# One written table for the order, the PSUM banks and the SBUF cells of an attention-and-MLP kernel

## The chip, the cores and the metric

The kernel runs on one core of one Trainium2 chip. The metric is the device time of one execution in microseconds (us). Three executions of the kernel before the change gave 410.02, 409.84 and 410.39 us; their median, 410.02 us, is the time before. The core has five instruction streams that run beside each other and meet only at semaphores: PE (TensorE, matrix products), ACT (ScalarE), DVE (VectorE), POOL (GpSimd) and SP (SyncE, which only issues DMAs here).

## The reference

A layer norm feeds a 16-head self-attention and a GELU MLP; the MLP, through SiLU, gates the attention's output, and the input is added. There are 2048 tokens of 448 numbers, heads of 28, and 1792 hidden columns. All inputs are bf16.

```python
xn = (x - mean(x)) / sqrt(var(x) + 1e-5)
qkv = (xn @ wqkv).reshape(B, S, 3, 16, 28)            # -> q, k, v by head
p = softmax(einsum("bhqd,bhkd->bhqk", q, k) * 28 ** -0.5)
s = einsum("bhqk,bhkd->bhqd", p, v) @ wo              # heads put side by side first
g = silu(gelu(xn @ w1 + b1, approximate=True) @ w2 + b2)
return x + s * g
```

## The kernel before, in words

**Scores.** The scores are cut into 1024 tiles of 128 keys by 512 queries, numbered m = 0 to 1023. A block is 64 tiles: one of four groups of four heads and one of four chunks of 512 queries; block b = m // 64, and m % 4 is the head in its group. PE makes a tile with a 32-row product, and four of these, one for each head, can stand side by side in PE's rows: this is a *row phase*. All other products of the main part use PE's columns: four products of 32 columns each side by side, a *slot*. A padded score tile (`p_alone`) is made in column mode, with a query operand that is zero for the other heads, and needs no change of mode. Changing between rows and columns costs PE time.

**Banks.** A product lands in PSUM, in one of eight banks that the program calls `ring`. Score tiles, projections, transposes and the accumulators of P·V all share these eight. A bank is free when what it holds has been read.

**Exponentials.** They are made on two engines.
- ScalarE reads two or three banks in one ACTIVATE (a *pair* or a *triple*) and writes bf16 to *cells* of P. Cells lie in several tensors whose first contents are dead by then, so in the profile they carry the names P, h, xnT and others.
- VectorE takes *groups* of four tiles with the same keys. A first pass (one `tensor_scalar` for each tile, multiply and add, written as uint16) makes bit patterns that are approximately the exponential. Two shifted copies of the whole group (128x2048, an integer added) follow, and P·V uses all three with weights of their own (`vs` holds the weighted V). A shifted copy is one DVE instruction (`tensor_scalar` on 128x2048 uint16) or two halves on POOL (`tensor_tensor` on 128x512 int32 with `shc`). The two copies can be *added* into one, which saves P·V a use: as one DVE instruction, or as accumulating DMAs that POOL issues (`p_expq`).

**P·V and the rest.** `t_pv` multiplies P with V, four heads a slot, and accumulates a block in one bank. When the bank is wanted elsewhere, or at the block's end, DVE moves the accumulator out (*evacuation*, `p_pv`, `p_epi`). Through the kernel's length the other work is spread between these: projections to q, k, v and to the MLP's hidden columns, whose last 64 rows are done either as full products or as two 32-row products that join a row phase ("joined"), GELU and tanh on ACT, SiLU by DVE and POOL (`p_silu`), the output projection and the output DMAs.

**The order.** `run` is a greedy scheduler with a cost model; it makes one list of operations (some 3,100 of them, numbered in order), each with its engine, the function that issues it, and `need`, the operations it must follow: R (reads what they wrote), W and A (overwrites what they wrote or read), X, and P and Q for the port. [...] `arrange` then permutes each engine's list by `ORD`: each number says how many of the remaining operations to step over. `place` sets the bank of some uses of banks by `BANKS` and works out the waits on banks anew, and `emit_all` writes each engine's program, with a semaphore wait ahead of an operation where its engine has not already waited for as much. `filler` puts products of `ident` and `zero` on PE where the scheduler sees nothing to do. A helper (line 258, in `_Eng`) issues every instruction, so nearly all profile lines have L258, and one goes by the names of tiles and by shapes.

**Beginning and end.** In the head, x and the weights come by DMA, and the statistics of the first four x tiles are made on DVE (`p_ln`) and, for tile 3, on ACT (`p_sums`: a copy that sums, operation 43, and a square that sums, 56). `p_ln2` makes the logarithm and the root for tiles 0 and 1 (half 0: operations 50, 53) and for 2 and 3 (half 1: 65, 69) on ACT, and the normalised tiles on DVE (58, 60 and 75, 72). PE transposes these; the transposed halves are copied out on ACT and DVE, `p_q0` makes the first q, and then the first scores can start. In the tail, `t_ones` and a reciprocal finish the softmax's sums of the last block, and the last outputs are multiplied, added and sent by SP, POOL and ACT.

Of the kernel before, what the change touches and what calls it, by code (L numbers as in the profile page):

```python
# [14 lines left out]
ORD = {  # L15
# [70 lines left out]
    ),  # L86
}
TO = ()
BANKS = {
# [9 lines left out]
H = 16  # L99
# [2933 lines left out]
```

## Time and profile before

| | |
|---|---|
| time of three runs | 410.02, 409.84, 410.39 us (median 410.02) |
| span of the profiled execution | 408.0 us, so 2.0 us of the median lie outside it |
| busy: PE, ACT, DVE, POOL | 395.1, 398.1, 343.5, 194.8 us |
| granted PE clock | 9 (tenths, 90% or more) in all 40 slices of the span |
| first exponential starts | 12.58 us |
| last exponential ends | 401.90 us |
| last DMA issued | 405.52 us |

The span is cut by these rows into a head of 12.6 us, a middle of 389.3 us in which ScalarE and VectorE make the exponentials, and a tail of 6.1 us. Busy time is the sum of the instructions' own durations with overlaps counted once; on PE and ACT an instruction starts before the one ahead of it has left the pipeline, so being busy isn't the same as having no time to spare, and the distance from one start to the next says more.

### The profile page before, as it was taken

The numbers are of one execution on the slowest core, as the hardware profiler recorded it, in microseconds if no ns is written. First come the engines' busy times: TensorE is split into PE (matmuls) and PEld (weight loads), VectorE is DVE, ScalarE is ACT, GpSimd is POOL, SyncE is SP. The second block draws the span as 40 slices with busy tenths as digits, with TensorE's granted clock in tenths as the row PEclk, the third lists the DMA queues.
The fourth block names the chain that finished last, engine by engine and source line by source line (L and its number), as shares of the span: only waits on it lengthen the run. The fifth ranks groups of instructions, "written<-read, shape, count | busy, mean of one in ns | idle before, by whom it ended". The sixth has DMA issues, their size and how long they took to land.

```text
span 408.0 us, 14601 instructions
## 1 busy us (share of the span) xinstructions
PE 395.1 (97%) x6157; PEld 144.6 (35%) x6157; DVE 343.5 (84%) x596; ACT 398.1 (98%) x409; POOL 194.8 (48%) x221
## 2 busy tenths in 40 slices
PE   6899999999999999999999999999999999999996
PEld 5443233333332333332223444332333323333363
DVE  8967688896679889989898127999998999798976
ACT  5999999999999999999999999999999999999995
POOL 7595457649982563254652231156156013555041
PEclk9999999999999999999999999999999999999999
DMA  8902110000101010100331100220010003200065
GB/s 244 305 2 42 4 31 2 16 20 19 29 3 31 2 25 11 34 2 2 77 116 30 30 3 6 55 53 15 18 34 2 4 31 57 64 20 21 14 114 134
DMA packets 18783, 17.54 MB, mean 43 GB/s; under 512 B 8941, under 2 KB 15421, under 8 KB 18686
## 3 DMA queue, kind: packets, MB, share of 16 engines
q1 hardware_dynamic: 16734, 13.55, 12.0%
q0 software_dynamic: 1008, 2.49, 3.8%
q8 instruction: 48, 0.79, 0.9%
q10 hardware_dynamic: 976, 0.57, 0.5%
q14 instruction: 17, 0.14, 0.1%
HBM read 12.54 MB, written 2.88 MB: 38 GB/s over the span
## 4 chain that ended last, share of the span: by engine, by line
PE 59%; ACT 28%; issue 7%; DVE 4%; DMA 1%; POOL 0%; ACTq 0%; DVEq 0%; POOLq 0%
PE ring L258 59%; ACT P L258 16%; ACT h L258 8%; ACT xnT L258 3%; DVE st L258 1%; DVE h L258 1%; DVE xnT L258 1%; DMA x_sb<-in_A_x_dram 1%; DVE vaug L258 0%; DVE x_sb L258 0%; ACT w L258 0%; DVE qT L258 0%; POOL h L258 0%; DVE mv L258 0%; DVE w L258 0%
## 5 line engine op out<-in xcount | busy, mean ns | idle before, releaser
L258 ACT ACTIVATE P<-ring 128x1024 bf16<-128x1024 f32 (+1 forms) x236 | 253.8, 1246 | 1.0 <-PE ring L258 1.0
L258 PE MATMUL ring<-qT,kT 32*128 32x512 bf16 (+2 forms) x1131 | 131.7, 359 | 4.2 <-ACT P L258 1.0
L258 ACT ACTIVATE h<-ring 128x1024 bf16<-128x1024 f32 (+2 forms) x93 | 101.3, 1204 | 2.0 <-PE ring L258 2.0
L258 PEld LDWEIGHTS ring<-qT,kT 32*128 32x128 bf16 x1131 | 36.3, 91 | 121.8 <-ACT P L258 48.1
L258 DVE TENSOR_SCALAR vaug<-ring 128x512 uint16<-128x512 f32 x92 | 60.8, 683 | 5.5 <-PE ring L258 4.8
L258 PE MATMUL ring<-xnT,w 128*32 128x512 bf16 (+1 forms) x880 | 65.3, 381 | 0.0
L258 PE MATMUL ring<-w,h 128*32 128x448 bf16 x896 | 58.5, 356 | 0.0
L258 PE MATMUL ring<-P,vaug 128*32 128x512 bf16 (+2 forms) x606 | 57.9, 351 | 0.2
L258 POOL TENSOR_TENSOR qT<-x_sb,E_sb 128x512 bf16<-128x512 f32 x15 | 17.4, 1162 | 64.6 <-DMA x_sb<-recs 38.0
L258 ACT ACTIVATE xnT<-ring 128x1024 bf16<-128x1024 f32 (+2 forms) x41 | 47.6, 1199 | 0.5 <-PE ring L258 0.5
L258 POOL TENSOR_TENSOR rc<-rs,mone 128x16 f32<-128x16 bf16 x11 | 33.3, 3023 | 28.7 <-DMA rs<-E_sb 14.6
L258 DVE TENSOR_SCALAR w<-ring 128x512 uint16<-128x512 f32 x52 | 34.5, 683 | 2.0 <-PE ring L258 1.7
L258 PEld LDWEIGHTS ring<-xnT,w 128*32 128x32 bf16 (+1 forms) x880 | 21.7, 96 | 28.0 <-issue 6.6
L258 PEld LDWEIGHTS ring<-w,h 128*32 128x32 bf16 x896 | 19.3, 95 | 24.4 <-issue 14.8
L258 PE MATMUL ring<-h,vaug 128*32 128x512 bf16 x201 | 25.1, 383 | 0.0
L258 PE MATMUL ring<-xnT,wq 128*32 128x512 bf16 (+2 forms) x240 | 22.6, 379 | 0.2 <-DVE w L258 0.2
L258 PEld LDWEIGHTS ring<-P,vaug 128*32 128x32 bf16 x606 | 17.3, 95 | 13.6 <-issue 7.4
L258 PE MATMUL ring<-xnT,wk 128*32 128x512 bf16 (+2 forms) x244 | 21.8, 379 | 0.3 <-DVE xnT L258 0.2
L258 DVE TENSOR_SCALAR h<-ring 128x512 uint16<-128x512 f32 x28 | 18.9, 685 | 3.3 <-PE ring L258 3.0
L258 POOL TENSOR_TENSOR qsq<-qT 128x512 bf16<-128x512 bf16 x12 | 13.0, 1079 | 17.0 <-DVE x_sb L258 13.9
L258 DVE CAST qT<-ring 128x512 bf16<-128x512 f32 x15 | 10.3, 688 | 12.7 <-PE ring L258 12.7
L258 DVE CAST h<-ring 128x512 bf16<-128x512 f32 x24 | 16.5, 688 | 4.8 <-PE ring L258 4.8
(207 smaller groups left out, 616.8 us busy)
## 6 DMA issues: line engine op xcount, KB each, us to landing
x_sb<-recs SPq DMA_DIRECT2D x60, 64.0 KB, 2.1
w<-in_B_w_dram SPq DMA_DIRECT2D x1, 1568.0 KB, 7.3
w<-in_B_w_dram SPq DMA_DIRECT2D x1, 1344.0 KB, 8.7
x_sb<-in_A_x_dram SPq DMA_DIRECT2D x2, 448.0 KB, 6.6
out_dram<-in_A_x_dram SPq DMA_DIRECT2D x2, 448.0 KB, 10.6
out_dram<-h POOLq DMA_DIRECT2D x4, 224.0 KB, 4.6
out_dram<-h SPq DMA_DIRECT2D x7, 112.0 KB, 4.4
xnT<-wq POOLq DMA_DIRECT2D x1, 512.0 KB, 6.6
```

What stands on the lines that cost most here:

```text
L258: return lambda *a, **k: f(*[real(x) for x in a], **{n: real(x) for n, x in k.items()})
```

## The change

One string, `PLAN`, with 3,586 entries, replaces `ORD`, `TO` and `BANKS`. It gives the order on all engines at once, the banks, and the cells that the exponentials go to. `run` still makes its list; operations that the plan names by number (`R`) are kept, with the bank that the plan gives. For the core of the work `arrange` makes the operations anew from the entries:

| entry | makes | before | after |
|---|---|---|---|
| X m,m(,m)/cells | exponential on ACT of one, two or three banks, of any equal spacing | 354 (286 pairs, 68 triples), 776 tiles | 358 (280 pairs, 67 triples, 11 singles), 772 tiles |
| S, C | score tile, padded score tile | 21 padded | 11 padded |
| A | first pass of a group's tile on DVE | 248 (62 groups) | 252 tiles (63 groups), 4 pairs of banks taken in one instruction |
| H, G | shifted copy on DVE, half of one on POOL | 92 and 64 | 54 and 144 |
| M | addition of two copies on DVE | 2, and 3 by DMA | 13 |
| V | product with V | 375 slots | 369 slots |
| E | evacuation of a P·V accumulator on DVE | 34 | 29 |
| P, J, Q | a projection's full products, its joined rests, its evacuation | 14 joined | 16 joined |

The waits come from a record of who last used each bank, cell and group place in the order of the plan (`take`, `room`, `begin`, `touch`). The fillers and the additions by DMA are dropped. DMA loads on SP and ACT keep their order. A POOL operation that wants the port waits for the last DVE operation in the plan's order that wants it. `emit_all` keeps for each operation only the largest wait of each semaphore. On ACT and DVE the first operations stand in another order (before: 43, 50, 53, 56, 65, 69, ...; after: 50, 53, 43, 56, 71, 65, 69, ...; on DVE before: 38, 42, 46, 52, 48, 58, ..., after: 38, 42, 46, 58, 60, 48, 52, ...), and at the end the last tanh (operation 3071) stands ahead of the last eight exponentials, and the output DMA 3075 ahead of 3062.

```diff
-ORD = {
-    'PE': (
-        0, 0, 0, 0, 0, 0, 0, 0, 0, 0, 0, 0, 0, 0, 0, 2, 2, 2, 0, 1, 1, 0, 19, 19, 1, 18, 2, 0, 0, 1, 3, 4, 0, 0, 0, 1, 0, 1, 0, 0, 0, 0, 0, 0, 3, 1,
...
-TO = ()
-BANKS = {
...
+PLAN = """
+    R2 R15 R16 R0 R4 R5 R6 R7 R3 R1 R35/7 R17 R38 R8 R21 R22 R264 R9 R24 R25 R26 R294 R18 R36/7 R19 R37/7 R42 R20 R39/7 R46 R40/7 R41/7 R44/7 R23
...
+    X803,804/0,16 V780,0/5 S895/3 S806/2 S805/1 S888/4 X805,806/1,4 A895/21 V816,0/5 V820,1/5 R2473 S890/0 S808/6 S807/7 R2544/3 R2545/3 X808,807/2,6
...
+    R3058/0 R3068/5 X1022,1023/10,13 R3059/0 R3064/0 R3070/4 R3081/1 R3072/4 R3073/4 R3065/2 R3082/1 R3066/2 R3076/5 R3085/1 R3086 R3037 R3069/0
+    R3079/4 R3084/5 R3088 R3074 R3067/2 R3087/2 R3083/0 R3089/2 R3090/0 R3093 R3091/0 R3031 R3054 R3025 R3075 R3062 R3094 R3092
+"""
...
+            elif t == "X":
+                bs = [sc[m][1] for m in a]
+                st = bs[1] - bs[0] if len(bs) > 1 else 1
+                src, dst = K.ring[:, bs[0]:bs[-1] + 1:st, :], cells(at)
+                need = [("R", H(sc[m][0])) for m in a]
+                for c in at:
+                    need += room([K.b_P[c]], cell, c)
+                o = new(ACT, lambda eng, src=src, dst=dst: eng.activation(dst, src, ACTF.Exp, scale=SM_SCALE), need, ("exp", a))
...
+            if o.port and o.E == POOL and port is not None:
+                o.need.append(("P", H(port)))
+            if o.port and o.E == DVE:
+                port = o
...
+                most = {}
                 for kind, (s, c) in o.need:
                     p = find[(id(s), c)]
-                    if kind == "Q" or kind == "P" and E == DVE or kind != "X" and E == PE and p.sem is self.evsem[PE]:
+                    if kind == "P" and E == DVE or kind != "X" and E == PE and p.sem is self.evsem[PE]:
                         continue
                     if done.get(id(p.sem), 0) < p.cnt:
                         done[id(p.sem)] = p.cnt
-                        self.prog[E].append(lambda eng, s=p.sem, c=p.cnt: eng.wait_ge(s, c))
+                        most[id(p.sem)] = p
+                for p in most.values():
+                    self.prog[E].append(lambda eng, s=p.sem, c=p.cnt: eng.wait_ge(s, c))
```

More of the change, by code (lines that the diff above doesn't have):

```diff
@@ L441, in arrange @@
-    def arrange(self):
-        seq = {}
-        for x in TO:
-            (self.to if len(x) > 2 else self.join)(*x)
-        self.chain_up()
-        for E, name in ((PE, "PE"), (ACT, "ACT"), (DVE, "DVE"), (POOL, "POOL"), (SP, "SP")):
-            lst = [o for o in self.ops if o.E == E]
-            at, left = [], list(range(len(lst)))
-            for d in ORD.get(name, ()):
-                at.append(left.pop(d))
-            seq[E] = [lst[i] for i in at + left]
-        self.place(seq)
-        self.emit_all(seq)
@@ L542, in chain_up @@
-    def chain_up(self):
-        chain = [o for o in self.ops if o.port and o.start is not None]
-        for at, o in sorted(self.put_port[::-1], key=lambda x: -x[0]):
-            chain.insert(at, o)
-        last = {}
-        for o in chain:
-            for E, kind in ((POOL if o.E == DVE else DVE, "P"), (o.E, "Q")):
-                if E in last:
-                    o.need.append((kind, (last[E].sem, last[E].cnt)))
-            last[o.E] = o
+        of = lambda h: K.by_h[(id(h[0]), h[1])]
@@ new lines, in arrange, with kind @@
+        K.number()
+        name = lambda o: o.fn.__qualname__.split(".<locals>.")[0].split(".")[-1] + ("" if o.fn.__qualname__.endswith("<lambda>") else "." + o.fn.__qualname__.split(".")[-1])
+        evac = {o.spec[1]: o for o in K.ops if o.spec and o.spec[0] == "ev" and not (o.spec[1][0] == "qk" and o.spec[1][2] == 0)}
+        keys = sorted(evac, key=str)
+        core = ("s", "sc", "exp", "a", "h", "evac", "last")
+        def kind(o):
+            s = o.spec
+            if name(o) == "filler.f" or o.kind == "x" or name(o) == "p_expq" and s is None:
+                return "gone"
+            if not s:
+                return "rest"
+            if s[0] == "pv":
+                return "rest" if s[2][0][0] // 64 == NBLK - 1 else "core"
+            if s[0] in core:
+                return "core"
+            if s[0] in ("pr", "ev") and s[1] in evac:
+                return s[0]
+            return "rest"
@@ new lines, in arrange @@
+        final = {o.spec[1]: o for o in K.ops if o.spec and o.spec[0] == "last"}
+        plan = [(x[0], *([int(z) for z in y.split(",") if z] for y in x[1:].split("/"))) for x in PLAN.split()]
+        ops, seq = {o.no: o for o in K.ops}, {E: [] for E in (PE, ACT, DVE, POOL, SP)}
+        full = {x[1][0] for x in plan if x[0] == "P" and x[1][1] == KT - 1}
+        merged = {x[1][0] for x in plan if x[0] == "M"}
+        grouped = {x[1][0] // 4 * 4 for x in plan if x[0] == "A"}
+        left = [sum(1 for x in plan if x[0] == "V" and x[1][0] // 64 == b) for b in range(NBLK)]
@@ new lines, in through @@
+        def through(p):
+            c, s = kd[id(p)], p.spec
+            if c == "rest" or c == "ev":
+                return [p]
+            if c == "pr":
+                return [evac[s[1]]]
+            if c == "core" and s[0] == "last":
+                return [p]
+            if c == "core" and s[0] in ("s", "sc", "pv"):
+                b = (s[1] if s[0] != "pv" else s[2][0])[0] // 64
+                return [final[b]] if b in final else []
+            return []
+        was = {id(o): list(o.need) for o in K.ops}
@@ new lines, in arrange @@
+        K.ops = [o for o in K.ops if kd[id(o)] == "rest" or o in list(evac.values()) or o in list(final.values())]
+        bank = {i: [] for i in range(NRING)}
+        cell, lane = {}, {}
+        sc, ex, ap, sh, pads, acc, burst, begun, part = {}, {}, {}, {}, {}, {}, {}, {}, set()
+        pr, done, last_pad, port, e1 = {}, set(), [], None, None
+        pad_of = [o for o in K.ops if name(o) == "p_pad" and o.E == SP]
+        shc = [o for o in K.ops if name(o) == "p_pad.f"][0]
+        vs = {o.spec[1:]: o for o in K.ops if o.spec and o.spec[0] == "vs"}
@@ new lines, in new, with take, cells @@
+        def new(E, fn, need, spec, port=False):
+            K.n_new += 1
+            o = K.op(E, fn, (K.evsem[E], 10 ** 6 + K.n_new), 1, (), (), "t", 0.1, 0.05, "", (), port, spec=spec)
+            o.need += need
+            return o
+        def take(i):
+            need = [("A" if p.E != PE else "W", H(p)) for p in bank[i]]
+            bank[i] = []
+            return need
+        def cells(cs):
+            reg, k = K.pslots[cs[0]]
+            n = len(cs)
+            st = cs[1] - cs[0] if n > 1 else 1
+            return reg[:, k:k + st * (n - 1) + 1:st, :]
@@ new lines, in used, with room @@
+        def used(x):
+            return [("A", H(p)) for p in [p for p in x if not p.spec or p.spec[0] not in ("exp", "a")] or x]
+        def room(toks, at, key):
+            if key in at:
+                return used(at[key])
+            need, seen = [], set()
+            for b in toks:
+                for h in first.get(id(b), ()):
+                    for p in through(of(h)):
+                        if id(p) not in seen:
+                            seen.add(id(p))
+                            need.append(("A", H(p)))
+            return need
@@ new lines, in touch, with score @@
+        def touch(u, o):
+            lane[u].append(o)
+            for c in lanes(u):
+                cell[c].append(o)
+        first = K.first_w
+        def score(m, b, pad):
+            b0, j, pc, _, _ = K.pieces(m)
+            g, c = b0 // C, b0 % C
+            tk = K.t_score([m], {m: K.ring[:, b, :]}, [], 1)
+            need = take(b)
+            if pad:
+                (t, _, _, _), = pc
+                fn = lambda eng: _mm(eng, K.ring[:, b, :], K.kT[:, g, 128 * t:128 * t + 128], K.qpad[:, :], True, True)
+                need.append(("R", H(pad_of[b0 - 2])))
+            else:
+                fn = tk.fn
+            for tok in tk.reads:
+                need += [("R", h) for h in writer[id(tok)].values()]
+            o = new(PE, fn, need, ("s", (m,)))
+            if pad:
+                pads.setdefault(b0, []).append(o)
+            bank[b] = [o]
+            sc[m] = (o, b)
+            return o
@@ L2169, in fall @@
             return ins
-        return _Task(PE, fall, rd, tok_of, 0.218 + 0.001 * len(fl), 0.17, prio, mode="row", rows=[p[2] for p in ps])
+        return _Task(PE, fall, rd, tok_of, 0.218 + 0.001 * len(fl), 0.17, prio, mode="row", rows=[p[2] for p in ps], spec=("s", tuple(ms)))
     def p_scores(self):
```

730 lines of the change are left out of this document (535 added, 195 removed), and 69 rows, old and new, of tables (BANKS, ORD).

## The prediction

> **What bounds the kernel now.** I read the page first, for the engines' shares and the chain of waits. The columns of the second line are busy microseconds, share of the span and instructions.
>
> ```profile
> span 408.0 us, 14601 instructions
> ## 1 busy us (share of the span) xinstructions
> PE 395.1 (97%) x6157; PEld 144.6 (35%) x6157; DVE 343.5 (84%) x596; ACT 398.1 (98%) x409; POOL 194.8 (48%) x221
> ```
>
> ```profile
> PE 59%; ACT 28%; issue 7%; DVE 4%; DMA 1%; POOL 0%; ACTq 0%; DVEq 0%; POOLq 0%
> ```
>
> ScalarE (ACT) and TensorE (PE) are both nearly full, and the chain goes through PE twice as long as through ACT. Next I asked for busy time by stretch: the middle, and the end up to the last exponential (columns: stretch, then busy time and instructions of PE, weight loads, DVE, ACT, POOL, then granted clock, DMA share, GB/s).
>
> ```profile
> 12.50:393.00 380.50, 375.05 (x5711) 131.62 (x5707) 321.75 (x530) 380.17 (x376) 181.13 (x187) 1.00 0.13 33
> 393.00:402.00 9.00, 8.66 (x288) 5.04 (x287) 8.01 (x20) 8.53 (x10) 2.81 (x5) 1.00 0.91 140
> ```
>
> Busy ACT says little, since consecutive ACTIVATEs overlap. So the next view is the timeline of ACT, where I take the time from one start to the next.
>
> ```profile
> 75.05 1.62 ACT L258 ACTIVATE P<-ring 128x1536 bf16<-128x1536 f32 x1
> 76.38 1.20 ACT L258 ACTIVATE h<-ring 128x1024 bf16<-128x1024 f32 x1
> 77.28 1.64 ACT L258 ACTIVATE P<-ring 128x1536 bf16<-128x1536 f32 x1
> ```
>
> A triple of banks (1536 columns) takes 1.33 us, a pair (1024) 0.90. Over all starts from 12.58 to 399.49 the medians are 1.331 and 0.904, so ScalarE pays 0.43 for each score tile beyond the first and some 0.05 for the instruction; a single is thus about 0.478 (estimate: 0.904 less 0.426). The span of exponentials begins and ends with these rows of the same view (the 399.49 row holds the last pair and the last triple, and ends at 401.90):
>
> ```profile
> 12.58 1.94 ACT L258 ACTIVATE P<-ring 128x1024 bf16<-128x1024 f32 x2 [0.36 <-PE ring L258]
> ```
>
> ```profile
> 392.32 2.17 ACT L258 ACTIVATE P<-ring 128x1024 bf16<-128x1024 f32 x2
> 394.95 3.77 ACT L258 ACTIVATE P<-ring 128x1024 bf16<-128x1024 f32 x4 [0.47 <-PE ring L258]
> 398.59 1.06 ACT L258 ACTIVATE xnT<-ring 128x1024 bf16<-128x1024 f32 x1
> 399.49 2.41 ACT L258 ACTIVATE P<-ring 128x1024 bf16<-128x1024 f32 x2
> 401.73 0.63 ACT L258 ACTIVATE w<-w 128x448 bf16<-128x448 bf16 x1
> ```
>
> From 12.58 to 401.73 are 389.15 us. In them lie 286 pairs and 68 triples of exponentials by the list of operations, and 12 GELUs of pair shape: 298 × 0.904 + 68 × 1.331 = 359.9. The other ACT work of that stretch is four groups (the view of groups by shape; busy, mean ns):
>
> ```profile
> L258 ACT ACTIVATE h<-h 128x1536 bf16<-128x1536 bf16 x8 | 11.9, 1486 | 0.0
> ```
>
> ```profile
> L258 ACT ACTIVATE w<-w 128x1792 bf16<-128x1792 bf16 x3 | 5.5, 1848 | 0.0
> L258 ACT ACTIVATE h<-h 128x1024 bf16<-128x1024 bf16 x4 | 4.4, 1096 | 0.0
> L258 ACT ACTIVATE w<-w 128x1344 bf16<-128x1344 bf16 x1 | 1.5, 1500 | 0.0
> L1375 ACT ACT_TABLE_LOAD x1 | 1.3, 1283 | 0.7 <-PEq L3018 0.7
> ```
>
> By their starts these 16 take 20.7 (each some 0.16 below its busy time) and two table loads 2.6. That makes 383.2, and **6.0 us are left in which ScalarE waits for scores**. One place is large: from 392.32 to 394.95 two pairs take 2.63 instead of 1.81, so 0.8 is lost there; the other 5.2 are spread in waits of a few tenths. What ends them is PE, which has about 375 us of work in 380. So ACT's own work is the floor, and PE's lateness is what lies above it.
>
> **The change part by part.** Counts are from the two orders, durations from the rows.
>
> *ScalarE's work.* 354 exponentials for 776 tiles become 358 for 772: 280 pairs, 67 triples, 11 singles. That is −6 × 0.904 − 1.331 + 11 × 0.478 = −1.5 us. ACT is the floor, so I count it in full.
>
> *TensorE's work.* The view is the timeline of PE.
>
> ```profile
> 153.01 0.39 PE L258 MATMUL ring<-vaug 128*32 128x512 bf16 x4
> 153.22 0.39 PE L258 MATMUL ring<-h,vs 128*32 128x512 bf16 x4
> 153.54 0.40 PE L258 MATMUL ring<-qT,kT 32*128 32x512 bf16 x4
> 153.87 0.40 PE L258 MATMUL ring<-w,vs 128*32 128x512 bf16 x4
> 154.09 0.39 PE L258 MATMUL ring<-P,vaug 128*32 128x512 bf16 x4
> ```
>
> A slot of four column products takes 0.216 (153.01 to 153.22, 153.87 to 154.09). A change to row products and back costs 0.10 and 0.11 more (153.22 to 153.54, 153.54 to 153.87). Slots of P·V fall from 375 to 369 (−1.3), padded score tiles from 21 to 11 (−2.2), row phases rise from 348 to 357 by my count (+1.9), runs of row phases fall from 315 to 309 (six pairs of switches, −1.3), and two more projections have their rests joined (−0.4): −3.3 us, or 0.9% of PE. The 84 filler matmuls that go lie where PE had nothing ready, so I count them at nothing; that cover gone, they would be worth at most 2 us of PE. Nothing of this is on the end directly; it shortens ACT's waits.
>
> *VectorE and GpSimd.* Each of the 63 groups (62 before) has two shifted copies of 128x2048. On DVE a copy takes 0.683, on POOL two halves of 1.040; an addition on DVE takes 1.212. The next rows are from the groups by shape.
>
> ```profile
> L258 DVE TENSOR_SCALAR h<-w 128x2048 uint16<-128x2048 uint16 x8 | 5.4, 683 | 0.0
> ```
>
> ```profile
> L258 DVE TENSOR_TENSOR x_sb<-x_sb 128x2048 bf16<-128x2048 bf16 x1 | 1.2, 1212 | 0.0
> ```
>
> ```profile
> L258 POOL TENSOR_TENSOR x_sb<-w,shc 128x512 int32<-128x512 int32 x12 | 12.2, 1040 | 6.5 <-PE ring L258 2.7 <-DVE x_sb L258 1.6 <-DVE w L258 1.4
> ```
>
> Copies on DVE go from 92 to 54, additions from 2 to 13, first passes from 248 tiles to 252, evacuations of the P·V bank from 34 to 29 (the last two at about 0.68 each, as the copies): −26.0 + 13.3 + 2.7 − 3.4 = −13 us of DVE, from 343 to 330. POOL has 144 halves instead of 64: +83 us, from 195 to 278 (68%). Three additions that were accumulating DMAs issued by POOL go with their issues; their transfers were beside other work. A product that needs a copy now waits for two POOL halves, 2.1 us instead of 0.7, and so its group's cells come free later; the order places the product later, hidden so long as the bank and the cells suffice. Every POOL port operation waits for the last DVE port operation that stands before it in the order, so POOL queues behind DVE. All this I count at 0, with the rival below as its price.
>
> *The head.* The loads are in the old order, but ACT now does the logarithm and root of half 0 (operations 50 and 53) ahead of the copy that sums x tile 3 (43), and DVE takes tile 2's statistics (48) behind the two normalisations (58, 60).
>
> ```profile
> 5.17 0.29 ACT L258 ACTIVATE lnv<-mv,epsc 128x2 f32<-128x2 f32 x1 [0.64 <-DVE mv L258]
> 5.50 0.20 ACT L258 ACTIVATE rstd<-lnv 128x2 f32<-128x2 f32 x1
> 5.61 0.65 ACT L258 ACTIVATE P<-x_sb,mv 128x448 bf16<-128x448 bf16 x1
> ```
>
> ```profile
> 6.94 0.20 ACT L258 ACTIVATE rstd<-lnv 128x2 f32<-128x2 f32 x1
> ```
>
> The logarithm cannot start before 5.17, so the sum (0.67 with its read-out) moves to 5.61 to 6.28 where the square now stands. DVE's small step on that sum (52) stands behind 48, which ends about 7.0; the square starts at 7.2 instead of 5.61, and the second root (it is the row of 6.94) comes, behind the transpose copy 71 that now precedes it, at about 8.8: 1.9 later. Downstream some of that was slack: by the same durations the second transposed half is 1.1 later, and the first exponential about 13.6 instead of 12.58. I take **+1.0**; it is between 0 (if the loads or the old slack set the start anyway) and 1.9.
>
> *The tail.* The tanh of the last output tile (operation 3071, the row of 401.73) moves ahead of the last eight exponentials: about +0.5 ahead of the last exponential (0.63 less the overlap of 0.16). Its POOL product and the DVE addition leave the last chain. In the tail's rows (DVE, then the last output's issue):
>
> ```profile
> 403.79 0.38 DVE L258 TENSOR_TENSOR h<-h,w 128x448 bf16<-128x448 bf16 x1
> 404.08 0.38 DVE L258 TENSOR_TENSOR h<-h 128x448 bf16<-128x448 bf16 x1
> ```
>
> ```profile
> 405.52 0.36 ACTq L258 DMA_DIRECT2D out_dram<-h  x1
> ```
>
> the addition holds the multiply up by 0.29, so −0.3 (403.79 to 404.08). What is late next is the multiply itself. Against it, SP's queue gets three or four output transfers together, with operation 3075 ahead of 3062; between −0.3 and +0.3, I take −0.3.
>
> *The waits.* The sum so far is −1.5 + 1.0 + 0.5 − 0.3 = **−0.3**. The rest is how the 6.0 us of waits change, which no row shows: the new order is its own. Its bounds are −6.0 (all go) and +6.0 (they double). PE's relief of 3.3 could at most take that much of the 5.2; the place at 392 to 395 (0.8) is rearranged altogether, as the last exponentials are now two and two with singles among them. I take all of the 0.8 and some 0.3 of the 5.2, that is 1.6: **−2.4**.
>
> Together −2.7 us. The profiled execution's span is 408.0, and 2.0 lie outside it to the median of 410.02; so 405.3 in the span, and **407.3 us** by the device. 0.2% is 0.8 us, about what a measurement of this kernel can tell from no change.
>
> [...] First the rows (one timeline, DVE and then POOL):
>
> ```profile
> 217.11 1.25 DVE L258 TENSOR_SCALAR kT<-vaug 128x2048 uint16<-128x2048 uint16 x1
> 218.28 1.53 DVE L258 TENSOR_SCALAR x_sb<-vaug 128x2048 uint16<-128x2048 uint16 x1
> ```
>
> ```profile
> 217.76 1.49 POOL L258 TENSOR_TENSOR qsq<-qT 128x512 bf16<-128x512 bf16 x1
> ```
>
> A copy that takes 0.683 alone took 1.25 and 1.53 where a POOL operation lay in between. [...]
>
> **The rivals.**
> *Slower: the port.* DVE keeps 54 copies and 13 additions that can meet a POOL half, and POOL is busy 68% instead of 48%. If each of the 67 is lengthened as that of 217.11 (by 0.57), DVE does 38 us more, which eats the 13 saved and 25 of its 59 free microseconds in the middle. First passes then leave their banks late and PE finds none. If that makes five more stalls like the 0.47 at 394.95, the waits grow by 2.4: −0.3 + 2.4 = +2.1, or 412.1. It decides from about 1.1 us of added waits on (two or three such stalls). For it speaks the pair of rows; against it, that POOL's wait for DVE's operation in the order can keep the two apart, and that most of the copies now run at 0.68.
> *No change: the terms cancel.* The new order has as many waits as the old one; PE's relief is lost to worse places. −0.3 gives 409.7.
> *A larger gain.* ACT hardly waits at all: 5 of 6.0 go, which gives 410.0 − 0.3 − 5 = 404.7. For it speaks that PE's work falls below ACT's; against it, that PE, busy 375 of 380 us now, would have to be on time at 358 places.
>
> **How the numbers follow.** The forecast (405.5 to 409.1) has 0.47, the larger gain 0.15, no change 0.17, the port 0.21. So faster 0.62, same 0.17, slower 0.21. The range reaches from the larger gain with no head delay (404.7 less about 0.7: 404.0) to the port's case (412.0).
>
> **What would show it.** In the changed kernel's profile: the first exponential near 13.6 (the head); groups of 128x1536 with 67 exponentials and a group of 128x512 with 11; DVE's total near 330 and POOL's near 278; copies of 128x2048 on DVE at a mean near 0.68 (the port rival: above 0.9); no row of a wait near the end like that of 394.95; from the last exponential's end to the span's end 5.8 instead of 6.1. The forecast is wrong if ACT's starts leave more than 6 us unexplained by its pitches, or if the first passes wait for cells instead of for scores, or if PE waits for a POOL half.

## The result and the profile after

The changed kernel is slower: median 416.14 us of four executions (415.73 to 417.3) against 409.93 us for the kernel before on the same chip, a ratio of 1.0153 with a 95% interval of 1.0138 to 1.0168. That is 6.2 us more, and outside the predicted range of 404.0 to 412.0. The profiled execution has a span of 414.3 us, 6.3 more than the 408.0 of before. The mean granted clock of PE was 0.999 in the profiled execution and 0.991 to 0.996 in the other three; runs 1, 3 and 4 below show such an execution's profile, with PE at half clock for 6.8 us near the end.

First the engines and the chain of waits on the page of the kernel after (columns as in the prediction):

```profile
span 414.3 us, 13763 instructions
## 1 busy us (share of the span) xinstructions
PE 394.1 (95%) x6015; PEld 144.1 (35%) x6015; DVE 337.0 (81%) x564; ACT 397.1 (96%) x413; POOL 272.1 (66%) x298
```

The work shrank as written: PE, DVE and ACT are each busy for less than before, only POOL for more. The span grew all the same, so what grew is waiting. The view of what ScalarE waits for (engine, tile, releaser: total, times, longest) of before and then of after:

```profile
ACT h L258 <- PE ring L258: 2.0, 2, 1.2
```

```profile
ACT P L258 <- PE ring L258: 1.0, 3, 0.5
```

```profile
ACT P L383 <- PE ring L383: 5.4, 5, 2.5
ACT h L383 <- PE ring L383: 3.7, 2, 2.4
```

The rows of P belong to the exponentials: their longest wait for PE was 0.5 us and is now 2.5, and the total is five times as large, in few, long pieces. (Both rows of h lie behind the last exponential.) The busy time by stretch says where (columns as in the prediction):

```profile
14.00:393.00 379.00, 371.25 (x5523) 129.52 (x5526) 313.16 (x495) 376.63 (x376) 257.24 (x263) 1.00 0.11 29
393.00:402.00 9.00, 6.68 (x208) 3.81 (x200) 5.08 (x11) 6.54 (x9) 2.44 (x3) 1.00 0.35 78
```

In the 9 us from 393 on, PE is busy 6.68 instead of 8.66 us, ACT 6.54 instead of 8.53. The account, from the first exponential's start (12.58, now 14.02) over the last one's end (401.90, now 407.01) to the span's end:

| term | predicted, us | measured in the profiled execution, us |
|---|---|---|
| head, to the first exponential | +1.0 | +1.44 |
| ScalarE's own work | −1.5 | −1.5 |
| the tanh put ahead | +0.5 | +0.5 |
| ScalarE's waits between | 6.0 to 3.6: −2.4 | 6.0 to about 10.4: +4.4 |
| tail, behind the last exponential | −0.3 | 6.1 to 7.3: +1.2 |
| sum | −2.7 | about +6.0 of the +6.3 |

The waits are found as the prediction did it: ACT's starts less the pitches 0.904, 1.331 and 0.478. They come to 1.0 at 23 us, 1.5 at 217 to 219, 2.6 at 395, and 5.3 in small ones elsewhere; before it was 0.8 at 392 to 395 and 5.2 elsewhere. The small ones did not change; three new long ones came.

**The head.** ACT's timeline of after:

```profile
5.50 0.56 ACT L383 ACTIVATE P<-x_sb 128x448 bf16<-128x448 bf16 x1
...
7.07 0.67 ACT L383 ACTIVATE P<-x_sb,mv 128x448 bf16<-128x448 bf16 x1 [0.92 <-DVE mv L383]
...
9.11 0.20 ACT L383 ACTIVATE rstd<-lnv 128x2 f32<-128x2 f32 x1
...
14.02 1.94 ACT L383 ACTIVATE P<-ring 128x1024 bf16<-128x1024 f32 x2 [0.75 <-PE ring L383]
```

The sum at 5.50, the square at 7.07 and the second root at 9.11 stand where the prediction put them (5.61, 7.2, 8.8). The text before the prediction, and the prediction, also say that the loads keep their order, and on SP they don't. The table moves four loads ahead, three rows of `wo` and that of b1h (3.5 KB in 1,792 elements). SP's queue, before and then after:

```profile
40.00 0.40 SPq L258 DMA_DIRECT2D b1h<-in_B_b_dram  x1
```

```profile
4.57 0.63 SPq L383 DMA_DIRECT2D b1h<-in_B_b_dram  x1
5.24 3.23 SPq L383 DMA_DIRECT2D x_sb<-in_A_x_dram  x2
```

The two x loads behind it take 3.23 us to issue; before, with nothing moved ahead of them, 1.06. DVE's timeline of after, in which the statistics of an x tile now wait for their load:

```profile
7.45 0.63 DVE L383 BATCH_NORM_STATS2 st<-x_sb 128x6 f32<-128x448 bf16 x1 [0.41 <-DMA x_sb<-in_A_x_dram]
```

The start at 14.02 is that of one execution: in the profiled executions of runs 3, 4, 5, 6, 8 and 10 below, which have the same head, it lies between 13.64 and 14.09.

**At 23 us.** POOL's and DVE's timelines of after:

```profile
20.63 2.43 POOL L383 TENSOR_TENSOR h<-h 128x1344 bf16<-128x1344 bf16 x1
```

```profile
21.55 1.95 DVE L383 TENSOR_SCALAR h<-x_sb,mv,rstd 128x448 bf16<-128x448 bf16 x2
```

POOL's square of the weights (operation 218) runs from 20.63 to 23.06; DVE's two normalisations start inside it and end at 23.50. They take 1.95 us; where POOL leaves them alone the pair takes 0.69 (third experiment). What PE makes of them is late, and ScalarE waits 0.81 at 25.01 (1.0 with the delays just before).

**At 217 us.** ACT's timeline of after:

```profile
221.00 2.37 ACT L383 ACTIVATE P<-ring 128x1024 bf16<-128x1024 f32 x2 [1.12 <-PE ring L383]
```

By the pitches 1.25 us are lost ahead of this row, and 0.25 ahead of the exponential before it. This wait is taken up at the end.

**At 395 us.** SP's queue, then POOL, PE and ACT of after:

```profile
389.99 0.30 SPq L383 DMA_DIRECT2D x_sb<-recs  x1
391.22 0.35 SPq L383 DMA_DIRECT2D h<-in_A_x_dram  x1
391.62 1.35 SPq L383 DMA_DIRECT2D x_sb<-recs  x3
```

```profile
396.53 1.15 POOL L383 TENSOR_TENSOR qT<-x_sb,E_sb 128x512 bf16<-128x512 f32 x1 [6.32 <-DMA x_sb<-recs]
```

```profile
397.74 0.37 PE L383 MATMUL ring<-wo,qT 128*32 128x448 bf16 x4 [2.32 <-POOL qT L383]
```

```profile
398.53 1.02 ACT L383 ACTIVATE P<-ring 128x1024 bf16<-128x1024 f32 x1 [2.46 <-PE ring L383]
```

Read downwards this is one chain. Four loads bring the reciprocals of a block's sums (`recs`) back. In SP's queue a load of x (operation 2984) stands behind the first; it waits for its place in `h` until 391.22, and so the other three reciprocals' loads wait behind it until 391.62. POOL's product needs all four and starts at 396.53. PE's product for the output projection (operation 3009) needs POOL's, and the next two score tiles stand behind it in PE's order: PE is idle 2.32 us, ScalarE 2.46.

**The tail.** PE's timeline of after:

```profile
406.89 0.56 PE L383 MATMUL ring<-P,one 128*32 128x128 bf16 x12
408.59 0.23 PE L383 MATMUL ring<-P,one 128*32 128x128 bf16 x1 [1.13 <-issue]
```

PE stops for 1.13 us in the middle of one operation, the products with ones that sum the last block; no semaphore is waited for there. The packets in the trace show what happens. The page has a DMA queue of the kind "instruction" whose packets go with PE's instructions:

```profile
q8 instruction: 47, 0.77, 0.7%
```

These are 47 packets of 16 KB, for the 12,030 matmuls and weight loads of PE: 256 to a packet, an estimate from these two counts (47 × 256 are 12,032). Counted back from the gap in such blocks, a packet starts behind each boundary that PE crosses, and its instructions are needed some 254 later. The four that start from 361.86 to 387.76 do so 0.5 to 0.6 us after the crossing. From 391 on, with the outputs and x in transfer, the last ones start 2.15, 2.17 and 2.94 us late (before: some 1.6 at most); the one whose boundary was crossed at 403.20 started at 406.13, and the gap ends at the first instruction that it brings. This stop belongs to the profiled execution. In those of runs 1, 3 and 4, whose order is the same there, PE does not stop at this place, the tail is 5.8, and time is lost to the half clock ahead of it instead.

### The profile page after: what moved, and what is told of

Same layout as the page of the kernel before. It is cut to its first block, busy times and chain, and to the rows that moved or that the text cites. A ratio compares the mean times of both kernels' runs of the same rounds, so it can differ in the third digit from the quotient of the medians.

```text
span 414.3 us, 13763 instructions
## 1 busy us (share of the span) xinstructions
PE 394.1 (95%) x6015; PEld 144.1 (35%) x6015; DVE 337.0 (81%) x564; ACT 397.1 (96%) x413; POOL 272.1 (66%) x298
## 4 chain that ended last, share of the span: by engine, by line
ACT 69%; PE 24%; DVE 2%; DMA 2%; issue 1%; SPq 1%; POOL 0%; DVEq 0%
ACT P L383 55%; PE ring L383 24%; ACT h L383 10%; ACT xnT L383 3%; DMA x_sb<-in_A_x_dram 1%; ACT w L383 1%; DVE h L383 1%; DMA x_sb<-recs 1%; SPq L383 1%; DVE st L383 0%; DVE qT L383 0%; POOL qT L383 0%; DVE w L383 0%; DVE kT L383 0%; ACT wq L383 0%
## 5 line engine op out<-in xcount | busy, mean ns | idle before, releaser
L383 ACT ACTIVATE P<-ring 128x1024 bf16<-128x1024 f32 (+2 forms) x301 | 299.6, 1166 | 5.5 <-PE ring L383 5.4
L383 PE MATMUL ring<-P,vaug 128*32 128x512 bf16 (+2 forms) x755 | 67.0, 350 | 0.0
L383 ACT ACTIVATE h<-ring 128x1024 bf16<-128x1024 f32 (+2 forms) x54 | 58.8, 1168 | 3.7 <-PE ring L383 3.7
L383 DVE TENSOR_SCALAR x_sb<-ring 128x512 uint16<-128x512 f32 (+1 forms) x59 | 40.3, 694 | 9.5 <-PE ring L383 9.0
L383 DVE TENSOR_SCALAR h<-ring 128x512 uint16<-128x512 f32 (+1 forms) x51 | 34.6, 694 | 1.9 <-PE ring L383 1.3
L383 DVE TENSOR_SCALAR w<-ring 128x512 uint16<-128x512 f32 (+1 forms) x47 | 32.0, 697 | 5.0 <-PE ring L383 4.4
L383 DVE TENSOR_SCALAR kT<-ring 128x512 uint16<-128x512 f32 x40 | 26.9, 685 | 5.8 <-PE ring L383 5.6
L383 ACT ACTIVATE xnT<-ring 128x1024 bf16<-128x1024 f32 (+2 forms) x19 | 22.2, 1231 | 0.5 <-PE ring L383 0.5
L383 PE MATMUL ring<-wo,qT 128*32 128x448 bf16 x256 | 18.1, 356 | 3.0 <-POOL qT L383 2.3
L383 PE MATMUL ring<-wv,xnT 128*32 128x112 bf16 (+2 forms) x508 | 19.4, 261 | 0.3 <-DVE h L383 0.2
```

The source lines that it names most:

```text
L383: return lambda *a, **k: f(*[real(x) for x in a], **{n: real(x) for n, x in k.items()})
```

## The experiments

My theory: the time was lost in few separate places (the head, 23 us, 217 us, the queue at 395 with its consequences), each a matter of order, and each can be taken away by moving a few entries. The rivals: one shared cause, such as DVE's and POOL's operations lengthened beside each other (the prediction's port), PE's total work, or DVE's additions; or a place that, mended, only hands its time to the next. Edits are of entries in `PLAN`. Each ratio is to the kernel before on the same chip; it is not exactly that of the two medians.

**1. The head in the old order.**

```diff
-  R50 ... R29 R265 R43 ... R58 R60 ... R48 ... R52 ... R55 R56 R71/0 R64 ... R65 R69 R63
+  R43 R50 ... R29 R265 ... R52 R48 R58 R55 R64 R60 ... R56 ... R65 R69 R63 R71/0
...
```

(R78, R85, R104, R114 and R122 go back likewise.)

> The changed kernel with the head's order of before on ACT and DVE (43 ahead of 50; 52 and 48 ahead of 58; 65, 69 and 63 ahead of 71; 78 and 85 behind 67), nothing else. Theory of places: the first exponential comes at about 13.0 instead of 14.02 (the early b1h load keeps some 0.4), and the time falls by about 1.0, to 415.1. Rival (what is won in one place is lost in the next wait): the first exponential comes earlier, but the last one ends where it did; 416.1 within 0.4.

Measured: 416.08 us (414.08 to 416.83), 1.0128 [1.01, 1.0156]. Its first exponential on ACT's timeline:

```profile
13.16 10.27 ACT L371 ACTIVATE P<-ring 128x1024 bf16<-128x1024 f32 x11
```

That is 0.86 earlier than 14.02 (0.48 to 0.93 earlier than the 13.64 to 14.09 of the same head), and 0.58 later than before. But the wait near 23 us grows from 1.03 to 1.38, and at the same exponential near 218 us only 0.37 is left of the 0.86. The head's order is worth some 0.5 to 0.9 at the head, and about half of it is lost again by 218 us, most of that at the wait near 23. The intervals of this run and of after overlap.

**2. The four loads later.**

```diff
-  R26 R294 R18 ... R29 R265 ... R266 ... R267 ... R32 X0,2/2,3
+  R26 R18 ... R29 ... R32 R294 R265 R266 R267 X0,2/2,3
```

> The changed kernel with four small loads (the transposed bias b1h, operation 294, and three rows of wo, 265 to 267) put behind the first w1 load in SP's queue, so that the x and wqkv loads are in the old order and as close as before. Theory of places: x's third load lands at about 6.8 instead of 7.42, the first exponential comes 0.3 to 0.5 earlier, 415.7. Rival: the order on ACT and DVE alone sets the head, 416.1 within 0.3.

Measured: 418.41 us (417.38 to 419.34), 1.0201 [1.0179, 1.0222], slower than after, which neither theory expected. The first exponential starts at 14.09: no gain. New waits of 1.74 at 16.8, 0.68 at 20.5 and 1.30 at 23.0 come, and this execution has PE at half clock there (busy time by stretch):

```profile
18.60:25.40 6.80, 6.80 (x79) 2.37 (x80) 4.88 (x9) 4.14 (x5) 5.41 (x8) 0.50 0.08 31
```

So this run does not tell what the early loads cost the head. A place between, or the old place at 40 us, was not tried.

**3. The square of the weights later.**

```diff
-  R172/5 R218 R187 ... R221/7 R214 R223/7
+  R172/5 R187 ... R221/7 R214 R218 R223/7
```

> The changed kernel with POOL's 2.4 us product (operation 218) put behind the small operations of the norms (195 to 214), as before. Theory of places: DVE's normalisation at 21.55 takes 0.4 instead of 1.64 since POOL no longer holds the port, ACT's wait of 1.03 at 23.07 goes, 415.1. Rival: DVE is late there for itself; the wait stays or moves on, 416.1 within 0.4.

Measured: 415.76 us (415.09 to 416.74), 1.0139 [1.012, 1.0157]. The normalisations on DVE's timeline, which took 1.95:

```profile
21.18 0.69 DVE L371 TENSOR_SCALAR h<-x_sb,mv,rstd 128x448 bf16<-128x448 bf16 x2
```

ScalarE's wait at 23 falls from 1.03 to 0.10, and two smaller ones come at 30.9 (0.37) and 35.9 (0.31). At 218 us the kernel is 0.85 ahead of after; but 0.38 of that is there at the first exponential already (13.64), which this edit does not touch, so the edit is worth about 0.5. The median shows 0.4. The cause of the wait at 23 is shown: POOL's product beside the pair of normalisations, which takes 1.95 us with it and 0.69 without. That POOL holds a port meanwhile is not shown. About half of the wait's 1.03 comes back in the two smaller ones.

**4. Another transfer at the end.**

```diff
-  R2859/1 R2702 R2791 ... R2917 S971/2
+  R2859/1 R2791 ... R2917 R2702 S971/2
```

> The changed kernel with the load of x's third part (operation 2702) behind the loads of the reciprocals (2791, 2792, 2917) in SP's queue, instead of ahead of them. Theory of places: the reciprocals' loads are issued near 390.3 instead of 391.6 to 392.6 and land by about 393 instead of 396.46, POOL's product follows, PE's wait of 2.3 at 397.74 and ACT's of 2.5 at 398.53 go or fall below 0.7; 414.0 (from 413.5 to 414.8). Rival (PE is bound there by its own work, and the outputs set the end): ACT's wait shrinks, but the end comes where it did, 415.7 or more.

Measured: 416.24 us (415.45 to 417.17), 1.0149 [1.0128, 1.017]. This was not the load that stands between them: the reciprocals' loads are issued as in after, so this is close to a second measurement of after, on the chip of runs 1 to 3. Its profiled execution had the half clock. Busy time from 397 to 404, of this run and then of after:

```profile
397.00:404.00 7.00, 6.47 (x136) 4.03 (x140) 2.90 (x6) 3.92 (x5) 2.27 (x4) 0.56 0.29 35
```

```profile
397.00:404.00 7.00, 6.09 (x180) 3.58 (x180) 4.72 (x9) 5.47 (x7) 3.46 (x5) 1.00 0.30 37
```

PE is busier and does 136 matmuls instead of 180; ScalarE does five instructions instead of seven.

**5. The load of x behind the reciprocals.**

```diff
-  R2939 R2984 R2940 R2941 ... R2942 R2977/7
+  R2939 R2940 R2941 ... R2942 R2984 R2977/7
```

> The changed kernel with the load of x that stands between the loads of the last reciprocals on SP (operation 2984; the run before had moved another load) put behind them (2939, 2940, 2941, 2942). Theory of places: the loads are issued from 390.0 to 391.2 instead of 390.0 and then 391.6 to 392.6, land by 393.3 instead of 396.46, POOL's product runs near 393.5, PE's gap of 2.0 to 2.3 near 397.5 goes, and with it the half clock (6.8 us at 0.5) that followed that gap in the runs of this chip; the last exponential ends 2.5 to 4.5 earlier, 413.0 (412.0 to 414.0). Rival (something else is late for the product, or PE's own work bounds the end): the gap moves or shrinks by less than 1, 415.3 or more.

Measured: 413.08 us (412.09 to 415.69), 1.0078 [1.0047, 1.0109], apart from the interval of after: 3 us by moving one entry. SP's queue and POOL:

```profile
389.95 1.70 SPq L371 DMA_DIRECT2D x_sb<-recs  x4
391.70 0.42 SPq L371 DMA_DIRECT2D h<-in_A_x_dram  x1
```

```profile
393.87 1.16 POOL L371 TENSOR_TENSOR qT<-x_sb,E_sb 128x512 bf16<-128x512 f32 x1 [3.80 <-DMA x_sb<-recs]
```

The product is 2.7 us earlier and PE has no gap there. ScalarE's waits near the end are one of 0.37 at 399.6. The stop in the tail is 0.31 us instead of 1.13, and PE stops for 0.42 at 400.79. The chain read at 395 is shown.

**6. As 5, with less output in transfer.** The output transfer of operation 2987, which POOL issues, is cut to one of its partitions, so that fewer bytes run beside the fetch of instructions.

```diff
+                if a[0] == 2987:
+                    o.fn = lambda eng, f=o.fn: f(_Cut(eng))    # dma_start(dst[0:1], src[0:1])
```

> As the kernel that has the x load behind the reciprocals' loads, and the last of the output transfers that POOL issues (operation 2987) carries one partition of 128 only, so most of two output tiles of every four there is left out. Theory that PE's instruction stream is fetched late when output transfers fill the DMA engines: PE's fetch near 403 to 406 starts within 1.6 of its crossing (2.9 late in the changed kernel), and no gap of PE above 0.5 in the middle of an operation follows; if that kernel without the cut shows such a gap, this one is 0.8 to 1.3 faster. Rival (the gap has another cause): a gap of about 1 stays.

Measured: 412.2 us (411.67 to 413.5), 1.0051 [1.0035, 1.0067]. The interval overlaps that of run 5, so the time decides nothing. In its packets the fetch that is beside the cut transfer starts 1.13 us after the crossing instead of 2.31, and PE does not stop at that instruction; the fetch before it, ahead of this transfer, is still about 2.3 late. That the transfers delay the fetch is thus supported by where it starts, not shown by a time. Its profiled execution, the slowest of six, has POOL's product at 395.38, 1.5 later than in run 5 with the same order of loads, and a wait of 1.37 at 395: what the moved load is worth differs between executions.

**7. Runs 1, 3 and 5 together, and one addition later near 217 us.**

```diff
   (as 1, 3 and 5)
-  R1232 M568 X548,549/2,5 ... X553,552/14,16 V568,1/7 V560,0/7 ... A559/3 X578,577/8,12 H560,2/1 ... V556,0/7
+  R1232 X548,549/2,5 ... X553,552/14,16 V560,0/7 ... A559/3 X578,577/8,12 M568 H560,2/1 ... V568,1/7 V556,0/7
```

> Four of the places at once: the head's order of before, POOL's 2.4 us product behind the norms' operations, the x load behind the reciprocals' loads, and the addition of group 568 with its product put behind the first passes of group 556 (DVE is busy without a pause from 212 to 222 there). Theory of places: first exponential near 13.2, waits at 23, 219 and 395 of 1.0, 1.2 and 2.6 each below 0.4, sum 0.8 + 1.0 + 0.9 + 2.5 to 4: 410.5 (409.3 to 412). Rival (what is won is lost to later waits): 413.5 or more.

Measured: 411.96 us (411.9 to 412.52), 1.0041 [1.0026, 1.0056]. The first exponential starts at 12.93, the last ends at 404.27, the span is 410.1. So moving entries alone brings back 4.6 of the 6.2 us (1.0153 less 1.0041 is 0.0112, of 410 us). The tail is 5.8, as predicted. What stays is near 217 us: a wait of 1.25 as before this edit, and a new one of 0.99 at 225.7. The fetches start at most 1.25 us late and PE does not stop for one.

**8. Less work for PE.** 28 products with V of second copies are left out (`V184,2`, `V188,2` and so on), so that the output lacks their part; 6.0 us of PE, all through the kernel.

```diff
-  V184,2/4
...
-  V880,2/0
```

> The changed kernel without 28 of the 47 products of a second shifted copy (blocks 2 to 13, spread evenly; that part of the output is left out): 28 slots of 0.216, 6.0 us of PE's work, nothing else. If ACT's small waits in the middle (5.3 us in all from 25 to 390 without the one at 219) come from the amount of PE's work, as the forecast of 2.4 us of gain for 3.3 us had it, they fall by 3 or more and the time with them, to 413. If they come from single operations that are late in the order, they fall by less than 1.2 and the time stays above 414.8.

Measured: 414.67 us (413.62 to 415.49), 1.0102 [1.0077, 1.0128]. Compared by stretches of 10 us, ScalarE's small waits from 25 to 390 us are those of after to within 0.1, and the wait of 1.25 at 217 stays. What differs is the end, where the long wait is 1.9 instead of 2.5, the profiled execution kept its full clock and the tail is 5.8:

```profile
ACT P L368 <- PE ring L368: 4.9, 5, 1.9
```

Taking 28 slots from PE (its busy time fell by 3.4) took nothing from the small waits. So the amount of PE's work does not make them; that single operations are late in the order is what is left. The time is just below the 414.8 set for this case.

**9. Runs 1 and 5, the square later still, and two scores ahead at 217 us.**

```diff
   (as 1 and 5)
-  R218 R187 ... R245 S47/0
+  R187 ... R245 R218 S47/0
-  S579/4 A557,558/3 S578/0 S580/5 ... X579,580,576/2,4,6
+  S579/4 S580/5 X579,580/2,4 A557,558/3 S578/0 ... X576/6
```

> The changed kernel with four edits of its table: the head's order of before; POOL's 2.4 us product behind the norms' operations and the relayouts (operation 245) as well; the x load behind the reciprocals' loads; and near 219 the exponentials of 579 and 580 first, as a pair, ahead of 578 and 577, with 576 alone behind (product and addition of group 568 where the changed kernel has them). Against the kernel with four edits (411.96) this lacks the wait of 0.99 at 225.7, should have that at 217.6 cut from 1.25 to about 0.5, and those at 30.3 and 35.5 (0.58 and 0.31) below 0.3 together. Theory of places: 409.9 (409.3 to 410.8), so the change's other edits together are worth about nothing beside before's 410.2. Rival (waits come back elsewhere): 411.5 or more.

Measured: 413.65 us (412.49 to 415.88), 1.0096 [1.0073, 1.0118]. The square is now too late; PE's timeline:

```profile
31.16 0.45 PE L371 MATMUL ring<-ones,h 128*128 128x1 bf16 x12 [1.34 <-POOL h L371]
```

ScalarE waits 1.18 at 29.9, 0.61 at 33.0 and 0.88 at 34.5, with PE at half clock from 32.6 to 36.0. Near 219 us 1.18 is lost all the same. The rival, a wait moved and not removed, holds for both edits.

**10. The gap at 395 filled.** The kernel after, with 84 products of `ident` and `zero` ahead of operation 3009.

```diff
-  R3008/1 R3009/1 S1007/3
+  R3008/1 F0/1 R3009/1 S1007/3
+            if t == "F":
...
+                [_mm(eng, acc[:, 0:128], K.zero[:, :], K.ident[:, :], False, True) for _ in range(21)]
```

> The changed kernel with 84 small products of zero (128x128, into the output projection's bank, adding nothing) ahead of the product that waits for POOL near 397.7; nothing else. If the half clock after that gap comes from PE standing idle for 2 us, no stretch of 0.5 follows near 397 in any execution (granted clock of the whole 0.999 or 1.000, not 0.990 to 0.996), ACT's wait of 2.5 stays, and the time is 415.2 (414.6 to 415.9) with less spread than 415.7 to 417.3. Rival (the clock falls for another reason, the count of the executions shows 0.991 to 0.996 as often as before): 416.1.

Measured: 414.98 us (414.76 to 415.25), 1.0115 [1.01, 1.013], apart from the interval of after (it just touches that of run 4), with the chain of run 5 unmended. The clock averaged over the whole run was 0.998 to 1.0 in all four executions (after: 0.991 to 0.999), and ScalarE's wait is still long. Busy time by stretch, and ScalarE's waits:

```profile
397.00:404.00 7.00, 6.36 (x224) 4.01 (x226) 4.18 (x9) 4.77 (x6) 3.75 (x5) 1.00 0.31 37
```

```profile
ACT P L371 <- PE ring L371: 6.0, 5, 3.0
```

So products that compute nothing save 1.6 us (0.0038 of 410), though ScalarE's wait is 3.0 here and not 2.5. For the executions with a lowered clock the clock explains it: in runs 1, 3 and 4 PE stands idle for 2.0 to 2.3 us and the clock falls to 0.5 for 6.8 us, while with the gap filled no execution is below 0.998. What the clock costs shows in run 4, where executions of one kernel at 0.996 took 415.45 and 415.63 us and those at 0.991 took 416.86 and 417.17. But the profiled execution of after kept its clock (0.999) and took 416.23, 1.0 more than that of this run (415.25); there it is the stop in the tail that differs (7.3 and 5.8).

**11. As 7, with scores ahead of the products at 217 us in place of the moved addition.**

```diff
   (as 1, 3 and 5)
-  V568,1/7 V560,0/7 ... A556/3 S579/4 A557,558/3 S578/0 S580/5 ... X579,580,576/2,4,6
+  A556/3 S579/4 S580/5 X579,580/2,4 V568,1/7 V560,0/7 ... A557,558/3 S578/0 ... X576/6
```

> The kernel with the head's order of before, POOL's 2.4 us product behind the norms' operations (214) and the x load behind the reciprocals' loads, without the move of group 568's addition; and near 219 the scores of 579 and 580 ahead of five slots of P.V on PE, their exponentials first. Theory of places: against the kernel with four edits (411.96) the wait of 0.99 at 225.7 goes, and the one at 217.6 falls from 1.25 to about 0.5, since PE makes the scores as soon as their banks are read: 410.3 (409.7 to 411.0). Rival (VectorE is the bound from 214 to 221, whatever PE does first): the waits there add up to 1.1 or more as before, 411.0 or more.

Measured: 412.05 us (411.74 to 413.52), 1.0052 [1.0038, 1.0066]: the rival. The 1.25 at 217.7 becomes 0.60, and 0.64, 0.33 and 0.40 follow by 226.2, which is 1.97 beside the 2.24 of run 7. ScalarE's waits for P have no long one left, and little is won:

```profile
ACT P L371 <- PE ring L371: 2.0, 6, 0.5
```

**12. As 11, without the three additions there.** The second copies are multiplied with V themselves.

```diff
-  M568 ... M564 M560
+  V568,2/7 ... V560,2/7 ... V564,2/7
```

> As the kernel with the scores of 579 and 580 first (412.05), but groups 568, 564 and 560 have their second copies multiplied with V on PE (three slots of 0.216 more) instead of being added on DVE (three additions of 1.22 each less, 3.7 us, all between 212 and 224). Theory that DVE's additions are what makes ACT wait there: ACT's waits from 210 to 230 fall from 2.45 to below 1.2, and the time to 410.9 (410.3 to 411.4). Rival (the additions fill time that DVE has, and banks held by first passes are what is short): the waits stay above 2.0 and the time is 412.0 within 0.4; the three slots on PE cost at most 0.6.

Measured: 412.49 us (412.38 to 414.33), 1.006 [1.0046, 1.0075]: the rival again, by its waits (the time is 0.1 above its 412.4). 3.1 us of waits stay between 210 and 230 us, although DVE now has much idle time there. Busy time in that stretch, and the longest gap on DVE's timeline:

```profile
210.00:230.00 20.00, 19.17 (x272) 7.07 (x272) 13.03 (x20) 17.79 (x18) 14.00 (x12) 1.00 0.02 3
```

```profile
224.01 0.69 DVE L371 CAST qT<-ring 128x512 bf16<-128x512 f32 x1 [3.46 <-PE ring L371]
```

The additions are not the cause. From 214.17 to 219.7, where the waits begin, DVE still reads one bank after another without a pause, so that the rival's other half, banks held by first passes, is not excluded.

## Why the prediction was wrong

**The step that failed first is the waits of ScalarE: −2.4 predicted, about +4.4 measured.** It rested on two thoughts. That PE's relief of 3.3 us would shorten the small waits: PE's busy time did fall (by 1.0), and the small waits went from 5.2 to 5.3; with 28 slots less (run 8) they did not move. And that the wait of 0.8 at 392 to 395 would go with its place: a longer one came there, 2.6 us. The prediction's bound for this term reached to +6.0, so its size was known to be open; the value taken had no row behind it. What would have had one is SP's queue: the prediction lists transfers that come together at the end, and did not ask what stands behind a load that has to wait for its place.

**"Fillers counted at nothing" is not refuted.** The prediction's reason was that PE had nothing else ready there. In run 10, 84 products of this kind in the gap at 395 were worth 1.6 us, with the clock at 0.998 to 1.0 instead of 0.991 to 0.999. But that is not what the change took away. In the kernel before the 84 stand in seven batches of 12, from 69.3 to 394.1 us, as their busy tenths in the 40 slices of the span show:

```profile
busy tenths in 40 slices 0000003033000000030007000000000000000030
```

Only 12 of them lay near 395, for some 0.3 us, and the gap of 2.3 us there is the new order's. No run took the fillers out of the kernel before.

**The head: +1.0 predicted, +1.44 measured.** ACT's order did what was worked out, to 0.3 us at each row; executions with this head start between 13.64 and 14.09, where 13.6 was forecast. Undoing the order gave 0.86 back (run 1). The step "the loads are in the old order" was false, as shown above. With the old order of ACT and DVE the first exponential is still 0.35 to 0.86 late (12.93 to 13.44 in runs 1, 7, 9, 11 and 12); that the four early loads cause this is argued from the wait at 7.45, not shown, since run 2 lost more elsewhere.

**The tail: −0.3 predicted, +1.2 measured.** The tail's own work came out as predicted: 5.8 in runs 7 and 11, and in runs 1, 3 and 4 too. The 1.13 us of PE's stop was in no term, and no row of before showed a stop in the middle of an operation. Neither such stops nor PE's clock near the end was in any term.

**The port rival had the right sign, by luck, and the wrong mechanism.** It asked for copies at a mean above 0.9, and the mean of the 54 is 0.714. Two groups of them, by shape:

```profile
L383 DVE TENSOR_SCALAR h<-x_sb 128x2048 uint16<-128x2048 uint16 x5 | 3.3, 683 | 0.0
L383 DVE TENSOR_SCALAR x_sb<-h 128x2048 uint16<-128x2048 uint16 x3 | 2.8, 948 | 0.0
```

Most groups stand at 0.683; four copies and two additions are long, and all lengthening of the copies and additions of 128x2048 together is 2.8 us (3.7 before). Where POOL beside DVE did cost, it was at 21.55, between a weight square and two normalisations that the prediction did not look at. By the third experiment the pair takes 0.69 without the square, so its price there is 1.26 us on DVE. `port` is the program's mark on operations of DVE and POOL. The rows show that some of these take longer beside each other (in before 1.25 and 1.53 us instead of 0.683, at 217.11 and 218.28); a shared port as the reason is shown by no run.

**What was right.** ScalarE's counts and pitches; the group of singles has its 11:

```profile
L383 ACT ACTIVATE P<-ring 128x512 bf16<-128x512 f32 x11 | 6.5, 645 | 0.0
```

POOL's total came to 272 (278 predicted), and DVE's to 337 (330 predicted, so it fell by half of the forecast 13). PE's busy time fell by 1.0 and not by 3.3; by run 8 the size of this term did not matter. Of the signs of error that the prediction set for itself, more than 6 us of ACT's time unexplained by its pitches came true. PE did wait for POOL too, but for a product ahead of the output projection, not for half of a copy.

**What stays open.** Of the 6.2 us, 4.6 went with moved entries (run 7). The rest, 1.7 us by that ratio, lies for the most part between 210 and 230 us: against before, run 11 has +0.4 at the head, −1.0 of ScalarE's work, +2.8 of waits and −0.3 in the tail, and 2.45 of its waits lie in that stretch. DVE's timeline of after there:

```profile
217.17 0.68 DVE L383 CAST qT<-ring 128x512 bf16<-128x512 f32 x1
217.77 0.68 DVE L383 TENSOR_SCALAR kT<-ring 128x512 uint16<-128x512 f32 x1
218.37 2.46 DVE L383 TENSOR_SCALAR w<-ring 128x512 uint16<-128x512 f32 x3
```

From 215.3 to 220.7 DVE reads one bank after another without a pause (an evacuation, first passes, and the output of a projection) while PE has no gap. Neither moving an addition (7), nor moving scores (9, 11), nor leaving out the additions (12) took it away. That PE's order there holds too much other work ahead of the scores is a guess; run 11 tried it for two score tiles only.

## What to carry to other kernels

When an order is replaced by another, the sums of busy time say what it could be worth, and single rows say what it will be: in each engine's and each DMA queue's new order, look for the entry that must wait and for what stands behind it, above all on the queue that no one counts as busy. Work that computes nothing may still be worth time (1.6 us for 84 products in run 10, with the clock at 0.998 to 1.0), so ask which gap it fills, and how long that gap is. And one long stall was mended by moving one entry (3 us for a load here), while at 217 us four tries only moved the wait.

## What the hardware showed that I had not expected

**Half clock after a gap.** In the profiled executions of runs 1, 3 and 4, PE's granted clock fell to 0.5 for 6.8 us, from 396.4 to 397.8 on, right behind or near the end of a gap of 2.0 to 2.3 us. In run 2 it was 0.5 for 6.8 us from 18.6 on, and for 3.4 us from 400.9 on, where PE was idle for 2.14 us between 397 and 404; in run 9 for 3.4 us from 32.6 on, behind a gap of 1.34. After's profiled execution has a gap of 2.32 at full clock (its other three executions show 0.991 to 0.996 over the run), and in run 8's PE waits 1.8 us for POOL's product, with the clock at 1.0 throughout. So the length of the gap alone does not decide, and no threshold shows. The traces of before and after have one change of the clock each, at 406.69 and 413.72, which is 399.36 and 406.19 us behind the clock's first record: 117 and 119 steps of 3.413 us, half the length of the longer falls. In such steps from after's first record (7.54), one ends at 396.66, inside the gap, and parts it into 1.24 and 1.08. That the gap had no fall behind it for this reason is a guess; no run tried it.

**Instructions arrived late beside transfers of data.** The fetch of a block of PE's instructions, which starts 0.5 to 0.6 us after the crossing for the four packets of after from 361.86 to 387.76, started up to 2.94 us late while outputs were in transfer. PE stood still for 1.13 us in after, 0.42 and 0.31 in run 5 and 0.85 in run 10, without a semaphore to wait for, and each time at the first instruction of a block by the count of 256. The DMA engines were busy for 0.71 to 0.80 of the time during the three latest fetches of after, and for 0.14 at the one before them (387.16). That the data cause the delay is argued, not shown: before had a share of 0.75 and 0.88 at its last two fetches, which started only some 1.5 to 1.6 us late.
